# Two plain blocks for three at the start, spare matmuls between, and the last block stored by halves, in a recurrence followed by a two-layer feed-forward

## The chip, the cores and the metric

One core of a Trainium2 chip. The metric is the time of one execution on the device in microseconds (us), as the median of several. The kernel before takes 2353.7 us. The time of an execution is some 1.8 us longer than the span in its trace (2354.12 and 2352.3 for the profiled execution of the kernel before).

## The reference, cut to what matters

```python
# x, f_logit: (4, 6080, 256); lower_bound: (256,)
f = lower_bound + (1 - lower_bound) * sigmoid(f_logit)
for t in range(6080):
    h = f[:, t] * h + (1 - f[:, t]) * x[:, t];  y[:, t] = h
h = y.reshape(24320, 256) @ w_in       # (256, 2048)
out = (h - tanh(h)) @ w_out            # (2048, 256)
```

The weights come as 64-bit floats, which the kernel turns into float32 on the vector and scalar engines while it starts.

## The kernel before

The 24320 tokens are cut in blocks of 512 and one of 256. A block goes through the recurrence (two scans on the vector engine), the first product, an elementwise polynomial for h - tanh(h), and the second product. Most blocks do both products with seven instead of eight products of quarter matrices (sums of quarters before and after, on the vector engine). These need sums of the weights too, so the first blocks are "plain", with eight products, while the weights still come in.

```python
sizes = [TB, HB] + [TB] * (N // TB - 1)      # TB = 512, HB = 256
PLAIN, TURNED = 3, 2                          # blocks 0, 1, 2 are plain
```

An opening table gives the order of every step until the steady order begins; each word is an operation on one block or one piece of weights (W fetch, c.. conversion, tf/tx transposes of a block's inputs, sc scan, F first product, t q w a g the elementwise part, S second product, A and B sums of weights):

```python
before = """
    W.0 df.0 dx.0 ce.0 cr.0 cm.0 cx.0 W.1 cs.0 cb.0 tf.0 cw.0 df.1 W.2 tx.0 sg.0
    f1.0 cm.1 ce.1 f0.0 v0.0 cx.1 cr.1 dx.1 cb.1 v1.0 W.3 sc0.0 tf.1 sc1.0 sg.1
    ... (cut)
```

The end: after the last block's output is summed and transposed, four stores of 128 KB go out on the SyncE queue (pieces of 256 bytes). Then a flag is made that says whether any value was too large for the polynomial; every engine reads it and branches over a general program if it is zero:

```python
def give(j):
    nc.vector.transpose(out=osb..., in_=acc[j, "C"]...)
    for i in range(G):                        # G = 4
        nc.sync.dma_start(out=dst[i], in_=osb[i * H : (i + 1) * H, 0:n])
# ... after all blocks:
nc.vector.reduce_max(out=worst[:], in_=flags[:], axis=X)
nc.tensor.matmul(most[0:1, 0, 0:1], lhsT=worst[:], rhs=ones[:], ...)
nc.vector.tensor_copy(out=flag[:], in_=most[0:1, 0, 0:1])
# ... then
seen = nc.values_load(flag...)
with tc.If(seen != 0):
    general()
```

Of the kernel before, what the change touches and what calls it, by code (L numbers as in the profile page):

```python
# [31 lines left out]
def kernel(  # L32
# [41 lines left out]
    sizes = [TB, HB] + [TB] * (N // TB - 1)  # L74
    PLAIN, TURNED = 3, 2
# [170 lines left out]
    def fast(ctx):  # L246
# [253 lines left out]
        def give(j):  # L500
            n = sizes[j] // H
            osb = opool.tile([P, TB // H, H * KC], FP32, name="osb", tag="osb")
            nc.vector.transpose(
                out=osb[:, 0:n].rearrange("p j (a k) -> p j k a", k=KC),
                in_=acc[j, "C"][:, 0 : n * KC * H].rearrange(
                    "p (k j b) -> p j k b", k=KC, b=H
                ),
            )
            dst = out[starts[j] : starts[j] + sizes[j], :].rearrange(
                "(j b) (i c) -> i b j c", b=H, i=G  # L510
            )
            for i in range(G):
                nc.sync.dma_start(
                    out=dst[i],
                    in_=osb[i * H : (i + 1) * H, 0:n],
                )

# [65 lines left out]
        def load(j, s):  # L583

            nat = spot(j, ("fn", "xn")[s])
            (nc.sync, nc.scalar)[s].dma_start(
                out=nat[:, 0 : sizes[j] // P],
                in_=srcs[s][starts[j] : starts[j] + sizes[j], :].rearrange(
                    "(n p) d -> p n d", p=P
                ),  # L590
            )
            nats[j, s] = nat
# [17 lines left out]
        def squash_banks(j):  # L610
            u = midpool.tile([P, TB // H, KC, H], FP32, name="fT")[:, 0 : sizes[j] // H]
            for k in range(KC):
                nc.scalar.activation(
                    out=u[:, :, k, :], in_=nats[j, "banks", 0][k],
                    func=AF.Sigmoid, scale=-1.0,
                )
            chan[j, 0] = u
# [11 lines left out]

        def p_first(j, u, s):  # L630

            nb = sizes[j]
            if (j, u) not in plain:
                plain[j, u] = hpool.tile([P, 2, 2, TB], FP32, name="h", tag="h")
            banks = []
            for c in range(2):
                name = "AABD"[2 * s + c]
                if (j, u) == (1, 0):
                    name = "Q" + "abcd"[2 * s + c]
                pool = ps_a if name == "A" else ps_b  # L640
                bank = pool.tile([P, TB], FP32, name=name, tag=name)
                banks.append(bank[:, 0:nb])
                for k in range(KC):
                    nc.tensor.matmul(  # L644
                        bank[:, 0:nb],
                        lhsT=w_in[u][:, 2 * k + s, c * P : (c + 1) * P],
                        rhs=ys[j][:, k, 0:nb],
                        start=(k == 0),
                        stop=(k == KC - 1),
                    )  # L650
            plain[j, u, s] = dict(banks=banks)
# [9 lines left out]
        def p_square(j, u, s):  # L661
            t = p_temp(j, u, s, "t")
            for c in range(2):
                nc.scalar.activation(
                    out=t[:, c], in_=plain[j, u, s]["banks"][c], func=AF.Square
# [14 lines left out]
        def p_shrink(j, u, s):  # L680
            for c in range(2):
                nc.vector.tensor_tensor(  # L682
                    out=plain[j, u][:, s, c, 0 : sizes[j]],
                    in0=plain[j, u, s]["banks"][c], in1=p_temp(j, u, s, "q")[:, c],
                    op=ALU.mult,
# [10 lines left out]
        def p_second(j, u, s):  # L696

            ns = sizes[j] // P
            if u == s == 0:
                acc[j] = [  # L700
                    ps_b.tile([P, 2, D], FP32, name=f"Q{b}", tag=f"Q{b}")
                    for b in ("ab", "c", "ab")[j]
# [12 lines left out]
        def p_give(j):  # L715
# [19 lines left out]
            tx=lambda j: turn_by_matmul(j, 1) if j < TURNED else steps["tx"](j),  # L735
            sg=lambda j: squash_banks(j) if j < TURNED else steps["sg"](j),
# [15 lines left out]
        for name in ("ce", "cr", "cx", "cm", "cs", "cb", "cw"):  # L752
# [5 lines left out]
            W.0 df.0 dx.0 ce.0 cr.0 cm.0 cx.0 W.1 cs.0 cb.0 tf.0 cw.0 df.1 W.2 tx.0 sg.0  # L758
            f1.0 cm.1 ce.1 f0.0 v0.0 cx.1 cr.1 dx.1 cb.1 v1.0 W.3 sc0.0 tf.1 sc1.0 sg.1
            f0.1 cs.1 f1.1 F.0.0.0 tx.1 df.2 cw.1 cm.2 cr.2 v1.1 v0.1 sc1.1 t.0.0.0  # L760
            sc0.1 ce.2 F.1.0.0 q.0.0.0 cs.2 cx.2 F.0.0.1 a.0.0.0 dx.2 t.1.0.0 cb.2
            w.0.0.0 g.0.0.0 q.1.0.0 W.4 w.1.0.0 F.1.0.1 a.1.0.0 t.0.0.1 cw.2 w.0.0.1
            g.1.0.0 F.0.1.0 q.0.0.1 ce.3 cm.3 cx.3 a.0.0.1 t.1.0.1 cb.3 cr.3 g.0.0.1
            q.1.0.1 W.5 w.1.0.1 cs.3 t.0.1.0 F.0.1.1 a.1.0.1 q.0.1.0 cw.3 w.0.1.0
            g.1.0.1 cr.4 a.0.1.0 S.0.0.0 t.0.1.1 cm.4 g.0.1.0 q.0.1.1 w.0.1.1 cs.4
            F.1.1.0 a.0.1.1 S.0.0.1 t.1.1.0 ce.4 q.1.1.0 g.0.1.1 cx.4 a.1.1.0 w.1.1.0
            cb.4 F.1.1.1 g.1.1.0 W.6 cw.4 S.1.0.0 t.1.1.1 q.1.1.1 cm.5 cr.5 F.0.2.0
            a.1.1.1 ce.5 w.1.1.1 g.1.1.1 cx.5 cs.5 F.0.2.1 cb.5 t.0.2.0 tf.2 W.7 w.0.2.0
            cw.5 q.0.2.0 S.1.0.1 t.0.2.1 a.0.2.0 cr.6 ce.6 df.3 S.0.1.0 tx.2 w.0.2.1
            g.0.2.0 q.0.2.1 sg.2 a.0.2.1 S.0.1.1 cx.6 cm.6 f0.2 g.0.2.1 f1.2 dx.3 cs.6  # L770
            F.1.2.0 cb.6 F.1.2.1 t.1.2.0 cm.7 W.8 cw.6 q.1.2.0 w.1.2.0 S.1.1.0 a.1.2.0
            t.1.2.1 ce.7 cr.7 S.1.1.1 g.1.2.0 q.1.2.1 cs.7 w.1.2.1 F.0.3.0 a.1.2.1 cx.7
            v1.2 g.1.2.1 cm.8 cb.7 F.0.3.1 t.0.3.0 v0.2 q.0.3.0 cw.7 w.0.3.0 a.0.3.0
            S.1.2.0 t.0.3.1 sc1.2 cr.8 S.0.2.0 g.0.3.0 q.0.3.1 ce.8 w.0.3.1 a.0.3.1 cx.8
            S.1.2.1 sc0.2 g.0.3.1 F.1.3.0 cb.8 F.1.3.1 t.1.3.0 cs.8 q.1.3.0 w.1.3.0
            S.0.2.1 a.1.3.0 t.1.3.1 cw.8 w.1.3.1 A.0.1 q.1.3.1 a.1.3.1 S.0.3.0 g.1.3.0
            g.1.3.1 A.0.3 F.2.0.0 A.1.1 A.0.2 tx.3 F.2.0.1 t.2.0.0 tf.3 q.2.0.0 A.1.2
            w.2.0.0 a.2.0.0 S.1.3.0 t.2.0.1 A.0.0 sg.3 S.1.3.1 g.2.0.0 w.2.0.1 v0.3
            F.2.1.0 q.2.0.1 B.0.0 v1.3 f0.3 a.2.0.1 f1.3 o.1 sc1.3 S.0.3.1 t.2.1.0
            g.2.0.1 q.2.1.0 sc0.3 w.2.1.0 a.2.1.0 F.2.1.1 o.0 m13.3 g.2.1.0 m2.3 F.2.2.0  # L780
            A.1.0 t.2.1.1 B.0.1 q.2.1.1 m4.3 A.1.3 w.2.1.1 a.2.1.1 S.2.0.0 t.2.2.0
            g.2.1.1 q.2.2.0 w.2.2.0 a.2.2.0 F.2.2.1 g.2.2.0 S.2.0.1 B.0.2 t.2.2.1
            q.2.2.1 w.2.2.1 a.2.2.1 F.2.3.0 B.1.0 g.2.2.1 F.2.3.1 t.2.3.0 w.2.3.0
            q.2.3.0 B.0.3 t.2.3.1 a.2.3.0 q.2.3.1 g.2.3.0 w.2.3.1 a.2.3.1 g.2.3.1
        """
        left = {
            ("Qb", 1): ["S.2.1.0"],
            ("Qd", 1): ["S.2.1.1"],
            ("Qa", 2): ["S.2.2.0"],
            ("Qc", 1): ["S.2.2.1"],  # L790
            ("Qc", 2): ["S.2.3.0"],
            ("Qd", 2): ["S.2.3.1", "B.1.1", "B.1.2", "B.1.3"],
            ("Qb", 2): ["o.2"],
        }

        def open_by(words):
            for word in words:
                name, *at = word.split(".")
                opening[name](*[int(i) for i in at])

        with tc.manual_schedule():
            nc.vector.memset(zeros[:], 0.0)
            nc.vector.memset(ones[:], 1.0)
            nc.gpsimd.dma_start(
                out=lb[:], in_=lower_bound.rearrange("(p k) -> p k", k=KC)
            )
            make_identity(nc, ident[:])

            bank = ps_b.tile([P, 2, HB], FP32, name="B", tag="B")
            for _ in range(3):  # L810
                nc.tensor.matmul(
                    bank[:], lhsT=zeros[:, 0:P], rhs=zeros[:], start=True, stop=True,
                    skip_group_check=True,
                )
            nc.vector.tensor_scalar(
                out=om[:], in0=lb[:], scalar1=-1.0, scalar2=1.0,
                op0=ALU.mult, op1=ALU.add,
            )
            nc.vector.tensor_scalar_add(out=nom[:], in0=lb[:], scalar1=-1.0)
            open_by(before.split())  # L820
            fetch(PLAIN + 1)

# [6 lines left out]
            for cycle in range(PLAIN, NBLK + 3):  # L829
                for name, u, at in turns:  # L830
                    j = cycle + at
                    if j == PLAIN - 1:
                        open_by(left.get((name, u), ()))
                    if not PLAIN <= j < NBLK:
                        continue
                    if u is None:
                        if (j, name) == (PLAIN, "m4"):
                            continue
                        steps[name](j)
                        if name == "tx" and j + 1 < NBLK and j > PLAIN:  # L840
# [3 lines left out]
            nc.vector.reduce_max(out=worst[:], in_=flags[:], axis=mybir.AxisListType.X)  # L844
            most = ps_b.tile([P, 2, HB], FP32, name="most", tag="D")
            nc.tensor.matmul(
                most[0:1, 0, 0:1], lhsT=worst[:], rhs=ones[:], start=True, stop=True
            )
# [130 lines left out]
```

## Time and profile before

| | kernel before |
|---|---|
| time, median of three | 2353.72 us |
| span in the trace | 2352.3 us |
| first useful product on TensorE | 14.44 us |
| last product ends | 2342.4 us |
| from there to the end ("the tail") | 9.98 us (9.9 in the prediction) |

TensorE is busy 99% of the span. A table like this is read from the two ends: in the middle TensorE never waits, so its time there is fixed by the number of products, and what can be won is a block's products, the opening, and the tail. The lines are shown and read in the prediction.

### The profile page before, as it was taken

To read this page: it belongs to the slowest core of one execution; us is meant where nothing else is said; L and a number is where in the kernel's file an instruction comes from. 1 tells how busy PE (TensorE), PEld (TensorE's weight loads), DVE (VectorE), ACT (ScalarE), POOL (GpSimd) and SP (SyncE) were. 2 spreads that over 40 slices of the span, in tenths; PEclk is the share of its full clock that TensorE was granted. 3 is DMA by queue.
4 is the path that set the end of the run, shared out by engine and by line. 5 is a ranking of instruction groups with operands and counts; after the bars stand their busy time and mean duration, and the time that the engine had idled before them with its cause. 6 is when DMAs were issued, how large, how long until landed. Compare 5 with 4: busy or idle time off the path is not lost.

```text
span 2352.3 us, 28494 instructions
## 1 busy us (share of the span) xinstructions
PE 2329.0 (99%) x10626; PEld 2019.8 (86%) x10626; DVE 2105.5 (90%) x2437; ACT 1794.1 (76%) x2681; POOL 1.4 (0%) x7
## 2 busy tenths in 40 slices
PE   8999999999999999999999999999999999999998
PEld 5768888888888888888888888888888888888887
DVE  8939998999899998999999998999989998999987
ACT  7648777777877777777777777777787777777775
POOL 0000000000000000000000000000000000000000
PEclk9999999999999999999999999999999999999999
DMA  5221111111211112111211112111111112111101
GB/s 171 50 35 28 27 39 34 37 27 28 46 33 31 27 32 41 36 28 27 44 29 37 27 27 46 36 28 28 36 37 36 28 28 45 30 34 28 27 10 29
DMA packets 296803, 85.04 MB, mean 36 GB/s; under 512 B 289744, under 2 KB 292560, under 8 KB 296656
## 3 DMA queue, kind: packets, MB, share of 16 engines
q1 hardware_dynamic: 295824, 82.35, 16.8%
q8 instruction: 85, 1.39, 0.2%
q10 hardware_dynamic: 800, 0.79, 0.1%
q14 instruction: 62, 0.51, 0.1%
q0 software_dynamic: 32, 0.00, 0.0%
HBM read 58.20 MB, written 24.90 MB: 35 GB/s over the span
## 4 chain that ended last, share of the span: by engine, by line
PE 98%; DVE 1%; DMA 0%; ACT 0%; issue 0%; DVEq 0%; POOLq 0%
PE A L383 26%; PE D L383 13%; PE Qd L466 13%; PE Qa L466 13%; PE Qb L466 13%; PE B L383 7%; PE Qc L466 7%; PE A L644 1%; PE Qa L706 1%; PE Qb L706 1%; PE B L644 1%; PE Qc L706 1%; PE D L644 1%; DVE q L676 0%; DMA lb<-in_lower_bound_dram 0%; DVE h L682 0%
## 5 line engine op out<-in xcount | busy, mean ns | idle before, releaser
L383 PE MATMUL A<-T,w_in 128*128 128x256 f32 x2160 | 547.0, 379 | 0.0
L383 PEld LDWEIGHTS A<-T,w_in 128*128 128x128 f32 x2160 | 410.3, 190 | 56.1 <-ACT B L395 0.3
L427 DVE TENSOR_TENSOR h<-h,q 128x1024 f32<-128x1024 f32 x360 | 428.1, 1221 | 3.1
L421 DVE SCALAR_TENSOR_TENSOR q<-q,t 128x1024 f32<-128x1024 f32 x360 | 430.5, 1217 | 0.0
L414 ACT ACTIVATE q<-t 128x1024 f32<-128x1024 f32 x360 | 374.4, 1053 | 44.3 <-DVE h L427 41.5
L411 ACT ACTIVATE t<-h 128x1024 f32<-128x1024 f32 x360 | 380.2, 1056 | 5.3 <-DVE h L398 2.6
L432 ACT ACTIVATE junk<-t 128x1024 bf16<-128x1024 f32 x360 | 379.7, 1055 | 1.5
L446 DVE TENSOR_TENSOR Tg<-h 128x1024 f32<-128x1024 f32 x360 | 340.7, 946 | 6.4
L466 PE MATMUL Qb<-h,w_out 128*128 128x256 f32 x1440 | 340.2, 379 | 0.0
L466 PEld LDWEIGHTS Qb<-h,w_out 128*128 128x128 f32 x1440 | 273.6, 190 | 37.2
L395 ACT COPY h<-B 128x512 f32<-128x512 f32 x180 | 104.8, 582 | 149.7 <-PE B L383 92.8
L466 PE MATMUL Qd<-Tg,w_out 128*128 128x256 f32 x720 | 214.1, 379 | 0.0
L466 PE MATMUL Qa<-Tg,w_out 128*128 128x256 f32 x720 | 214.1, 379 | 0.0
L466 PE MATMUL Qd<-h,w_out 128*128 128x256 f32 x720 | 214.1, 379 | 0.0
L466 PE MATMUL Qa<-h,w_out 128*128 128x256 f32 x720 | 214.1, 379 | 0.0
L398 DVE TENSOR_TENSOR h<-D,r 128x512 f32<-128x512 f32 x180 | 124.2, 690 | 100.4 <-PE D L383 99.4
L395 ACT COPY h<-A 128x512 f32<-128x512 f32 x180 | 104.9, 583 | 133.5 <-PE A L383 122.4
L398 DVE TENSOR_TENSOR h<-A,r 128x512 f32<-128x512 f32 x180 | 123.6, 687 | 82.1 <-PE A L383 50.8
L383 PE MATMUL A<-y,w_in 128*128 128x256 f32 x720 | 185.7, 380 | 0.0
L383 PE MATMUL D<-T,w_in 128*128 128x256 f32 x720 | 185.7, 380 | 0.0
L395 ACT COPY r<-A 128x512 f32<-128x512 f32 x180 | 104.9, 583 | 105.1 <-PE A L383 105.1
L383 PE MATMUL B<-y,w_in 128*128 128x256 f32 x720 | 184.8, 379 | 0.0
(114 smaller groups left out, 3173.7 us busy)
## 6 DMA issues: line engine op xcount, KB each, us to landing
fn<-in_f_logit_dram SPq DMA_DIRECT2D x184, 128.0 KB, 3.2
xn<-in_x_dram SPq DMA_DIRECT2D x184, 128.0 KB, 3.3
out_dram<-osb SPq DMA_DIRECT2D x180, 128.0 KB, 2.8
raw<-in_moe_w_in_dram SPq DMA_DIRECT2D x8, 512.0 KB, 5.2
raw<-in_moe_w_out_dram SPq DMA_DIRECT2D x8, 512.0 KB, 5.0
out_dram<-osb SPq DMA_DIRECT2D x2, 512.0 KB, 3.4
xn<-in_x_dram ACTq DMA_DIRECT2D x1, 512.0 KB, 4.0
fn<-in_f_logit_dram SPq DMA_DIRECT2D x1, 512.0 KB, 6.2
```

What stands on the lines that cost most here:

```text
L383: nc.tensor.matmul(ps[:, c], lhsT=w_in[u][:, slot, c * P : (c + 1) * P], rhs=mixes[j][right], start=start and c == 0, stop=True, skip_grou ...
L395: nc.scalar.copy(out=dst, in_=piece(n, bank))
L398: nc.vector.tensor_tensor(out=piece(n, "h")[:, q], in0=piece(n, bank), in1=piece(n, r), op=ALU.add)
L411: nc.scalar.activation(out=half(n, i, "t"), in_=half(n, i), func=AF.Square)
L414: nc.scalar.activation(out=half(n, i, "q"), in_=half(n, i, "t"), func=AF.Square, scale=RA, bias=RB,)
L421: nc.vector.scalar_tensor_tensor(out=q, in0=q, scalar=RC, in1=t, op0=ALU.add, op1=ALU.mult)
L427: nc.vector.tensor_tensor(out=h, in0=h, in1=q, op=ALU.mult)
L432: nc.scalar.activation(out=junk[:, :, :, 0 : st[n]["hb"]], in_=t, func=AF.Relu, bias=-TINY, accum_out=flags[:, 2 * n + i : 2 * n + i + 1],)
L446: nc.vector.tensor_tensor(out=o, in0=a, in1=b, op=ALU.subtract)
L466: nc.tensor.matmul(acc[j, part][:, r, 0 : st[n]["hb"]], lhsT=w_out[u][:, slot, c * P : (c + 1) * P], rhs=piece(n, right)[:, q, c], start=( ...
L644: nc.tensor.matmul(bank[:, 0:nb], lhsT=w_in[u][:, 2 * k + s, c * P : (c + 1) * P], rhs=ys[j][:, k, 0:nb], start=(k == 0), stop=(k == KC - 1),)
L706: nc.tensor.matmul(acc[j][i // 2][:, i % 2].rearrange("p (k m) -> p k m", k=2), lhsT=plain[j, u][:, s, c, i * P : (i + 1) * P], rhs=w_out[ ...
```

## The change

Its intent: one plain block fewer, so that one more block has seven products for eight; a smaller first block, so that TensorE starts earlier; the next block already interleaved with the last plain work; spare matmuls of zeros so that TensorE's clock stays up; and a shorter end. Beside this, the first inputs are all loaded by SyncE's queue, the lower bound by ScalarE's, and the sigmoid table is loaded at the start. The core of the diff (the new table of about 330 words, bank names and helpers are cut):

```diff
-    sizes = [TB, HB] + [TB] * (N // TB - 1)
-    PLAIN, TURNED = 3, 2
+    sizes = [HB] + [TB] * (N // TB)
+    PLAIN, TURNED = 2, 2
...
+        def end(j):
+            for half, slot, r in ((0, 2, 1), (1, 1, 0)):
+                nc.vector.tensor_tensor(
+                    out=C[:, slot], in0=acc[j, 3][:, r, 0:hb], in1=C[:, slot], op=ALU.add)
+                turn_out(j, (slot,))
+                send(j, half)                 # four stores of 64 KB, SyncE queue
...
+            K1.7 W.0 df.0 ce.0 cr.0 dx.0 cm.0 tf.0 cx.0 W.1 cs.0 tx.0 sg0.0 cb.0 K1.4
+            sg1.0 df.1 v0.0 f0.0 cw.0 f1.0 v1.0 dx.1 ce.1 tf.1 sc1.0 cx.1 sc0.0 W.2 cr.1
+            cm.1 tx.1 sg1.1 cb.1 sg0.1 cs.1 F.0.0.0 f0.1 v1.1 f1.1 dx.2 v0.1 K1.4 cw.1
+            t.0.0.0 sc0.1 q.0.0.0 F.0.0.1 w.0.0.0 W.3 sc1.1 cr.2 K1.2 a.0.0.0 t.0.0.1
+            F.1.0.0 ...
...
+        def keep_busy(n):                     # the word K1.n
+            for _ in range(n):
+                nc.tensor.matmul(busy[:], lhsT=zeros (bf16), rhs=zeros (bf16, 512 wide), ...)
...
-            nc.gpsimd.dma_start(out=lb[:], ...)
+            nc.scalar.dma_start(out=lb[:], ...)
...
+                        if (name, j) == ("o1", NBLK - 1):
+                            tc.mark_branch_hint_location("general", "LikelyTaken")
+                            nc.vector.reduce_max(out=worst[:], in_=flags[:], ...)
+                        if j == NBLK - 1 and name in ("o4", "otr"):
+                            if name == "o4":
+                                sum_up()      # flag: matmul and ScalarE copy, now early
+                                end(j)
+                            continue
...
+                        if (name, j) == ("o3", NBLK - 1):
+                            turn_out(j, (0, 3))
-    with tc.If(seen != 0):
+    with tc.If(seen != 0, label="general"):
```

## The prediction

> **What bounds the kernel now.** I read the page first, then the chain of waits in order of time, then the opening, the change of method and the end instruction by instruction.
>
> ```profile
> PE 2329.0 (99%) x10626; PEld 2019.8 (86%) x10626; DVE 2105.5 (90%) x2437; ACT 1794.1 (76%) x2681; POOL 1.4 (0%) x7
> ```
>
> TensorE is busy 99% of a span of 2352.3 us, so the steady part has nothing to win except matmuls that go away. The vector engine at 90% is the next bound, close behind. The chain of waits gives the period of a block of 512 tokens by seven products:
>
> ```profile
> 258.28 1.73 PE A L383 x8
> ...
> 354.97 1.73 PE A L383 x8
> ```
>
> These are two equal places two blocks apart: 96.69 us, 48.35 us for a block. It agrees with the counts: 224 matmul records a block, about 0.216 us apart. The reader is to see that every microsecond that is not 48.35 times a number of blocks lies at the two ends. The waits of TensorE in the first 200 us, and the busy times of the engines in four stretches (columns: stretch, its length, then PE, PEld, DVE, ACT and POOL busy with counts, clock, DMA share, GB/s):
>
> ```profile
> PE B L825 <- DVE h L682: 4.0, 1, 4.0
> PE A L644 <- DVE y L227: 3.8, 1, 3.8
> PE Qa L644 <- DVE y L227: 2.4, 1, 2.4
> ```
>
> ```profile
> 14.44:37.85 23.41, 19.95 (x52) 10.17 (x53) 20.36 (x30) 18.23 (x31) 0.00 (x0) 0.93 0.65 141
> 37.85:137.90 100.05, 100.05 (x369) 69.73 (x367) 86.30 (x136) 66.60 (x113) 0.00 (x0) 1.00 0.28 62
> 137.90:147.90 10.00, 6.03 (x14) 4.14 (x14) 6.75 (x8) 3.74 (x6) 0.00 (x0) 0.66 0.38 65
> 147.90:193.00 45.10, 45.10 (x210) 39.45 (x209) 20.54 (x25) 25.42 (x42) 0.00 (x0) 1.00 0.11 21
> ```
>
> All those waits are for the vector engine. It is the limit from 14.44 to 37.85 us and again at the change of method near 140 us; between and after, TensorE never waits, and from 147.9 to 193 us the vector engine stands idle more than half the time. The opening and the change of method, from the timeline:
>
> ```profile
> 6.35 0.17 DVE L815 TENSOR_SCALAR om<-lb 128x2 f32<-128x2 f32 x1 [4.93 <-DMA lb<-in_lower_bound_dram]
> ...
> 7.60 1.28 ACT L613 ACT_TABLE_LOAD   x1
> ...
> 14.44 5.40 PE L644 MATMUL A<-y,w_in 128*128 128x512 f32 x8 [3.83 <-DVE y L227]
> ...
> 141.89 2.08 PE L825 MATMUL B<-zeros 128*128 128x512 f32 x2 [3.97 <-DVE h L682]
> ...
> 143.76 1.91 PE L383 MATMUL A<-y,w_in 128*128 128x256 f32 x4
> ```
>
> The first useful product starts at 14.44 us. The last plain product of the opening table begins at 136.04 us and lasts 1.88; the bank B is cleared only at 141.89, and the first of the seven products runs at 143.76 at half clock. The end, from the chain:
>
> ```profile
> 2340.64 1.74 PE Qd L466 x8
> 2342.38 0.02 issue
> 2342.40 0.70 DVE C L498
> 2343.10 0.02 issue
> 2343.13 1.25 DVE osb L503
> ...
> 2345.18 0.15 DVE flag L849
> ```
>
> TensorE ends at 2342.4; 9.9 us remain. Of these 2.0 are the sum and the transposition, 0.8 the flag, and some 7 the last four stores and the branch over the general program.
>
> **What the Trainium skill says.** "TensorE: Matmul & The Clock Gate", Part 1, "What's actually happening": after an idle window of about 3.4 us the array runs at half clock until it has been busy for about as long. The trace agrees: after the two waits of 3.8 and 4.0 us the granted clock falls (0.93 and 0.66 in the rows above), and eight 512-wide records take 5.40 us where the chain later shows 3.43. "ScalarE: Activation LUTs", "What ACT_TABLE_LOAD costs", gives 1283 ns for the load itself; the trace has 1.28 us, twice, the second just before the first sigmoid. "DMA: Bandwidth & Descriptors", "SWDGE vs HWDGE vs iDMA", calls transfers from the scalar engine faster to set up than those from GpSimd; the trace has only the GpSimd one for the lower bound, 5.1 us from issue to landing. "Runtime: NRT & Kernel Launch", "Instruction fetch mechanics": a taken branch to a page that is not loaded waits for its fetch by DMA; in the last 6.8 us nine instruction packets move, which agrees.
>
> **The change part by part.**
>
> *A block turned from plain to seven products.* Plain block of 512: per quarter of the weights the first layer is 16 records of 512 columns (3.43 for eight in the chain, so 6.87) and the second 32 of 256 (6.9); four quarters are 55.1 us. Seven products: 48.35. The new kernel has 46 such blocks for 45, one plain 512 for two, and the 256 (27.6) in both. TensorE gains 6.75 us.
>
> *What TensorE's end consists of, before.* 45 x 48.35 = 2175.8, plain work 55.1 x 2 + 27.6 = 137.8, together 2313.6. The remainder to 2342.4 is 28.8: start 14.44; waits 2.45 and 1.0; two pairs of transposes between products 0.6; 6.0 from the end of the plain products (137.75) to the first of the seven; half clock 1.7 (14.77 to 18.2, half of it lost) and 2.1 (143.76 to 147.9). Sum 28.3, so the books close.
>
> *Start.* 256 tokens first: the two scans cost about 0.65 each for 1.15, the factors v 0.4 for 0.65. The vector engine's work ahead of the first product falls from 7.9 to 6.4 us by my sum of durations. The lower bound comes through the scalar engine's queue and its two small results are made there, so the vector engine need not wait until 6.35; fewer bytes (1.0 MB for 1.5) are asked for ahead of the first weights; the sigmoid table is loaded in the idle start, which takes 1.28 us off the scalar engine's way. From about 5.3 us: 5.8 of vector work less memsets gives 10.4 if nothing stalls, 11.4 if the first weights still land at 6.1. I take 10.8: 3.6 gained.
>
> *Opening from there.* I summed the durations of each word of the new table: between the first product and the first of the seven products the vector engine has 68.2 us of work, TensorE 72.7 with its spare matmuls. Up to the first second-layer product it is 19.4 against 18.4. The same sum for the kernel before gives 20.4 vector us where the window shows 20.36, so the sums hold; there that stretch took 23.4, the vector engine busy 87%. At the same share the new stretch takes 22.3, so about 4 us of wait or spare, and I add 1 for half clock that the spare matmuls (zeros, bfloat16, 0.22 us each, 11 early and 6 later) don't prevent: 5.
>
> *Change of method.* In the new table the second layer of the plain block still runs among the first products of the block after, and the clear of B comes while others wait; 0.9 for the clear and 2 for waits, where before it was 6.0 + 2.1. New remainder: 10.8 + 5 + 2.9 = 18.7. TensorE's end: 46 x 48.35 + 55.1 + 27.6 + 18.7 = 2325.5, 16.9 earlier.
>
> *End.* The last block's sums r=1 and r=0 are made, turned and stored apart, two of the four transpositions done before. First store possible 0.8 us after the last product for 2.0. But eight issues of some 0.4 to 0.5 us stand for four on one queue, and the same count of small packets moves, so not all of the 1.2 arrives. The flag is made while the sums wait, so its load and the branch no longer come last, hinted or not. I take 8.2 for 9.9: 1.7 gained.
>
> Sum: 6.75 (the block) + 3.6 (start) + 6.5 (opening and change of method: 14.4 before, 7.9 after) + 1.7 (end) = 18.6. Span 2352.3 - 18.6 = 2333.7; the time stood 1.4 us above the span, so 2335 us.
>
> **The rivals.** First: the vector engine becomes the bound. The plain block that goes had 18.6 us of vector work (eight times 1.13 + 1.2) beside its recurrence for 55.1 of TensorE; a block by seven products has about 44 for 48.35 (915 us busy in 1000 of the steady part), and all the conversion of the weights and their sums stay. From the first product to the end of the new table I count 110.3 vector us for 115.9 TensorE us. The slack that the old kernel had from 147.9 to 193 us is gone. For it: the rows at 14.44 and 137.9. Against it: 5.6 us are still free in the table, and steady blocks give back 4 us each. If it idles 10% of the opening, TensorE waits 6 to 10 us more: 2341 to 2345. Second: the order in the new table is so good that the waits vanish and the spare matmuls keep the clock full: 4 to 6 us less, 2329 to 2331. Third: the last stores are bound by their packets and by the issuing queue, and the halves bring nothing: 1.7 us more, 2337. Fourth: the spare matmuls sit before useful ones and delay them; 17 by 0.22 are 3.7 us at most at full clock, of which I have most counted in the 5.
>
> **Range and chances.** Mostly the vector engine in the opening decides: minus 6 to plus 7 around 2335, 2329 to 2342. For 2% the time would have to fall by 47 us; all that is not useful work in the old kernel is 28.8 + 9.9 us, and with the 6.75 the whole is 45.5. So faster by over 2%: 0.01; within 2%: 0.985; slower: 0.005.
>
> **What would show it.** The first first-layer product near 10.8 us; no granted clock under 0.9 near 140 us; waits of TensorE in the first 150 us of about 5 to 7 us in all; the period of 48.35 us unchanged; TensorE's end near 2325.5 and about 8 us behind it. Wrong, if the period changes, if waits for the vector engine in the first 150 us exceed 12 us, or if the last 8 us are still 10.

## The result, and the profile after

The changed kernel takes 2335.9 us (median of 4 runs, 2334.3 to 2336.5), the kernel before in the same rounds 2353.65. The ratio is 0.992, 95% interval 0.9903 to 0.9937, which is within 2%, as forecast. A ratio here is the mean time of one kernel's runs over that of the other's of the same rounds, so not quite the ratio of the medians. The prediction was 2335. But two of its terms were wrong, in opposite directions, as the trace shows: TensorE ends at 2321.5 us where 2325.5 was predicted, and the tail is 13.2 us where 8.2 was.

The first line of the page after:

```profile
PE 2318.4 (99%) x10669; PEld 2024.6 (87%) x10669; DVE 2121.2 (91%) x2450; ACT 1800.4 (77%) x2685; POOL 0.7 (0%) x6
```

The waits of TensorE in the first 200 us after, all of them; the second is for the memset at the very start:

```profile
PE Qa L623 <- DMA fn<-in_f_logit_dram: 1.5, 1, 1.5
PE B L849 <- DVE ones L875: 1.5, 1, 1.5
```

Before, the same view had three waits of 2.4 to 4 us and one of 1.0 us for the vector engine. After, there is none for it but that memset. The busy times of the engines in stretches of the new opening (stretch, length, then PE, PEld, DVE, ACT and POOL, clock, DMA share, GB/s):

```profile
12.43:30.93 18.50, 18.50 (x64) 11.23 (x63) 18.23 (x25) 16.27 (x28) 0.00 (x0) 1.00 0.82 185
30.93:90.00 59.07, 59.07 (x234) 44.11 (x233) 56.44 (x81) 41.95 (x67) 0.00 (x0) 1.00 0.30 88
90.00:100.00 10.00, 10.00 (x48) 8.81 (x47) 7.67 (x17) 6.18 (x11) 0.00 (x0) 1.00 0.01 2
100.00:145.00 45.00, 45.00 (x210) 39.44 (x209) 43.48 (x60) 38.25 (x61) 0.00 (x0) 1.00 0.32 65
```

From the first product (12.43) to the first second-layer product (30.93) the vector engine is busy 18.23 of 18.50 us, 99%. In the old opening the same stretch was busy to 87%. Up to the scans of the second block the vector engine sets the pace, as the first rival feared, but it hardly idles, and TensorE, filled up with spare matmuls, shows no wait.

The timeline of the new opening, cut to the lines that matter:

```profile
5.28 0.43 DVE L134 TENSOR_SCALAR e<-raw 128x512 int32<-128x512 int32 x1 [3.88 <-DMA raw<-in_moe_w_in_dram]
...
12.43 1.89 PE L678 MATMUL A<-y,w_in 128*128 128x256 f32 x8
...
14.62 2.45 DVE L227 TENSOR_TENSOR_SCAN y<-f,y,v 128x512 f32<-128x512 f32 x2
...
17.18 1.88 PE L678 MATMUL Qa<-y,w_in 128*128 128x512 f32 x4
...
84.36 1.02 PE L859 MATMUL B<-zeros 128*128 128x512 f32 x2
85.22 1.03 PE L383 MATMUL A<-y,w_in 128*128 128x256 f32 x4
```

The scans of the second block end at 17.07 us (14.62 + 2.45), and its first product starts at 17.18. The change of method at 84 us, which cost 6 us of waiting and 2 of slow clock before, costs only the 0.86 us of the clear. The period of a block is the same as before, 48.34 us, between equal places in the chain of waits:

```profile
285.78 1.73 PE A L383 x8
...
334.12 1.73 PE A L383 x8
```

The end, from the timeline: the vector engine's last work, then the row of SyncE's queue, the eight last stores put together.

```profile
2320.89 0.77 DVE L512 STREAM_TRANSPOSE osb<-C 128x256 f32<-128x256 f32 x2
...
2321.58 0.39 DVE L535 TENSOR_TENSOR C<-Qd,C 128x256 f32<-128x256 f32 x1
...
2322.80 0.45 DVE L512 STREAM_TRANSPOSE osb<-C 128x256 f32<-128x256 f32 x1
```

```profile
2322.48 7.24 SPq L521 DMA_DIRECT2D out_dram<-osb  x8
```

Before, the four stores were issued in 2.17 us, also from the timeline:

```profile
2344.40 2.17 SPq L513 DMA_DIRECT2D out_dram<-osb  x4
```

The halves do go out earlier after TensorE's end: the first at 1.0 us for 2.0. But eight issues take 7.24 us, so the last one is out at 8.2 us after TensorE's end; before it was out at 4.2. After its last issue SyncE still loads the flag, branches and runs a row of closing waits. From the end of that issue to the end of the program are 5.0 us here, 5.8 before, and 5.0 to 6.6 in all fourteen traces. In the changed kernel the last store has landed at 9.6 us, while SyncE is back from its branch at 11.3. So the tail follows SyncE's last issue. One by one, as the trace has them (start after TensorE's last product, length):

```
 before  +2.04 0.32   +2.68 0.32   +3.05 0.51   +3.61 0.60
 after   +0.97 0.32   +1.33 0.44   +1.83 2.20   +4.07 0.45
         +4.62 0.41   +5.07 0.46   +5.58 2.14   +7.76 0.45
 16 KB instruction packets on queue 8:
 before  +5.62 for 1.35            +9.18 for 0.96
 after   +1.96 for 1.64            +5.79 for 1.53
```

Six issues take 0.32 to 0.46 us, two take 2.2. Both slow ones lie over a large instruction fetch. The DMA view (queue, packets, MB, share of the engines' time) shows the same: first the 2.3 us of the first slow issue in the new kernel, then the 2.4 us of the four issues in the kernel before, which have no packet of queue 8:

```profile
q1 hardware_dynamic: 525, 0.13, 25.2%
q8 instruction: 1, 0.02, 4.5%
q14 instruction: 2, 0.02, 3.3%
```

```profile
q1 hardware_dynamic: 880, 0.22, 41.2%
q14 instruction: 1, 0.01, 0.8%
```

Whose fetches are they? The 16 KB packets of queue 8 come every 27.6 us (median) in the steady part, and TensorE issues 448 recorded instructions in 48.35 us, so 256 in 27.6: that would be 64 bytes for each. At the end, the first of the two large packets starts 1.0 to 2.0 us after TensorE's branch in all fourteen traces, wherever that branch is. So I take them for TensorE's, which is an inference. That an issue is held where it meets such a packet also shows away from the end. In the steady part of the changed kernel's trace SyncE issues 500 transfers. The 28 during which a packet of queue 8 moves take 0.72 us on average and up to 1.64; the other 472 take 0.47, and none over 0.86 (counted in the packed trace). In the new kernel the flag is made before the last sums, so TensorE branches at 0.93 us after its last product (before: 3.74) and its two fetches fall among the stores.

### The profile page after: what moved, and what is told of

It is laid out like the page before. It is cut to its first block, busy times and chain, and to the rows that moved or that the text cites. A ratio compares the mean times of both kernels' runs of the same rounds, so it can differ in the third digit from the quotient of the medians.

```text
span 2334.7 us, 28635 instructions
## 1 busy us (share of the span) xinstructions
PE 2318.4 (99%) x10669; PEld 2024.6 (87%) x10669; DVE 2121.2 (91%) x2450; ACT 1800.4 (77%) x2685; POOL 0.7 (0%) x6
## 4 chain that ended last, share of the span: by engine, by line
PE 99%; DMA 0%; SPq 0%; DVE 0%; issue 0%; DVEq 0%
PE A L383 27%; PE Qa L466 14%; PE Qb L466 14%; PE D L383 14%; PE Qd L466 14%; PE Qc L466 7%; PE B L383 7%; PE Qc L745 1%; PE Qa L745 1%; PE Qb L745 1%; PE A L678 1%; PE D L678 0%; PE Qd L678 0%; DMA xn<-in_x_dram 0%; PE B L678 0%; PE Qc L678 0%
## 5 line engine op out<-in xcount | busy, mean ns | idle before, releaser
L383 PE MATMUL A<-T,w_in 128*128 128x256 f32 x2208 | 558.8, 379 | 0.0
L383 PEld LDWEIGHTS A<-T,w_in 128*128 128x128 f32 x2208 | 419.5, 190 | 57.0
L427 DVE TENSOR_TENSOR h<-h,q 128x1024 f32<-128x1024 f32 x368 | 437.3, 1219 | 3.1
L421 DVE SCALAR_TENSOR_TENSOR q<-q,t 128x1024 f32<-128x1024 f32 x368 | 439.8, 1215 | 0.0
L414 ACT ACTIVATE q<-t 128x1024 f32<-128x1024 f32 x368 | 382.9, 1053 | 46.3 <-DVE h L427 43.4
L411 ACT ACTIVATE t<-h 128x1024 f32<-128x1024 f32 x368 | 388.6, 1056 | 3.1 <-DVE h L398 0.3
L432 ACT ACTIVATE junk<-t 128x1024 bf16<-128x1024 f32 x368 | 388.2, 1055 | 1.5
L446 DVE TENSOR_TENSOR Tg<-h 128x1024 f32<-128x1024 f32 x368 | 347.8, 945 | 6.3
L466 PE MATMUL Qb<-h,w_out 128*128 128x256 f32 x1472 | 347.7, 379 | 0.0
L383 PE MATMUL D<-y,w_in 128*128 128x256 f32 x736 | 188.9, 379 | 0.0
```

The costliest lines, as they stand in the source:

```text
L383: nc.tensor.matmul(ps[:, c], lhsT=w_in[u][:, slot, c * P : (c + 1) * P], rhs=mixes[j][right], start=start and c == 0, stop=True, skip_grou ...
L411: nc.scalar.activation(out=half(n, i, "t"), in_=half(n, i), func=AF.Square)
L414: nc.scalar.activation(out=half(n, i, "q"), in_=half(n, i, "t"), func=AF.Square, scale=RA, bias=RB,)
L421: nc.vector.scalar_tensor_tensor(out=q, in0=q, scalar=RC, in1=t, op0=ALU.add, op1=ALU.mult)
L427: nc.vector.tensor_tensor(out=h, in0=h, in1=q, op=ALU.mult)
L432: nc.scalar.activation(out=junk[:, :, :, 0 : st[n]["hb"]], in_=t, func=AF.Relu, bias=-TINY, accum_out=flags[:, 2 * n + i : 2 * n + i + 1],)
```

## The experiments

All outputs are right. Each kernel had five timed runs; the kernel before, in the same rounds, had medians from 2353.78 to 2354.02. Runs 1 to 4, 5 to 8 and 9 to 12 shared one chip each, three chips in all. "TensorE's end" and "tail" are of each one's profiled execution.

| run | time, median | range | TensorE's end | tail |
|---|---|---|---|---|
| changed, first trace | 2335.9 | 2334.3-2336.5 | 2321.5 | 13.2 |
| new opening, old end | 2334.23 | 2333.6-2335.3 | 2323.6 | 9.8 |
| whole store, early flag | 2335.01 | 2333.63-2336.01 | 2323.7 | 10.5 |
| halves, late flag, no hint | 2335.75 | 2335.52-2336.7 | 2322.5 | 11.3 |
| no hint | 2338.29 | 2336.62-2338.4 | 2323.7 | 12.7 |
| halves on two queues | 2334.18 | 2333.92-2335.13 | 2322.1 | 11.1 |
| no spare matmuls | 2336.97 | 2336.02-2337.66 | 2323.1 | 12.1 |
| product ahead of transposes | 2339.1 | 2337.92-2340.15 | 2325.3 | 13.1 |
| old opening, new end | 2357.15 | 2355.58-2359.8 | 2341.9 | 13.4 |
| changed, again | 2336.43 | 2335.71-2338.65 | 2324.0 | 12.8 |
| two queues, flag after sums | 2333.08 | 2333.03-2334.57 | 2323.6 | 9.1 |
| the same, no spare | 2334.04 | 2333.46-2334.28 | 2322.9 | 9.4 |
| the same, whole store | 2333.41 | 2333.0-2334.86 | 2323.1 | 9.5 |

The five times of one kernel spread by 0.8 to 4.2 us (those of the control by 2.9), so two medians about 1 us apart are not told apart here.

My theory for the end: the early flag brings the branch's fetches into the stores. Rivals: eight issues are too many in any case; the hint makes the fetches. For the opening: the vector engine's chain to the second block's scans decides, against the moment of the first product.

**1. New opening, old end.**

```diff
-  early reduce_max, hint, sum_up(), end(j), turn_out(j, (0, 3))
+  one sum, one transposition, four stores; then reduce_max, matmul, copy as before
```

> The new opening with the old end: one sum, one transposition, four stores, flag last, no hint. The changed kernel's trace has TensorE ending at 2321.5 us and 13.2 us after it, where the kernel before had 9.9. Theory A (the new end costs what the opening won too much): TensorE ends at 2321.5 again, 9.9 us behind it, span near 2331.4, time near 2332.6, 3.3 below the changed kernel. Rival (the longer tail only moved there because the opening shifted the stores against the instruction fetches): the tail stays at 12 to 13 us and the time near 2336.

The tail is 9.8 us and the four issues take 2.18 us (SyncE's row of the timeline, below): theory A. The time is 1.6 us above the number expected, because TensorE ended at 2323.6, not 2321.5; that is the subject of the control below.

```profile
2325.66 2.18 SPq L521 DMA_DIRECT2D out_dram<-osb  x4
```

**2. Whole store, early flag and hint kept.**

```diff
-                                end(j)
-                            turn_out(j, (0, 3))
+  (the ordinary o4 and give, four stores of 128 KB)
```

> The changed kernel with the early flag and the hint, but one sum, one transposition and four stores of 128 KB. Theory A1 (an issue on the SyncE queue stalls some 1.7 us when it meets one of the two large instruction fetches of TensorE's branch): one of four issues is stalled, issues end about 5.7 us after TensorE, tail 10.5 to 11.5, time about 2333.5 to 2334. Rival A2 (only the number of issues counts, each has its chance of a slow one): no stall, tail 9 to 9.5, time near 2332.

Tail 10.5. The four issues take 3.29 us; two are slow (1.30 and 1.04 us) and each lies over or beside a packet of queue 8 (at 1.98 for 1.27, and 5.80 for 1.09 us after TensorE's end; the slow issues began at 2.40 and 4.28 us). The second slow one ends at 5.3, ahead of the second of these packets; a packet of 8 KB on queue 14 lies over it (at 4.31 for 0.48), but whether that one holds it I did not test. The tail fits theory A1.

**3. Halves, late flag.**

```diff
-  reduce_max at o1 and sum_up() ahead of end(j)
+  reduce_max and sum_up() after the last transposition
-  the hint and the label of the branch
```

> The changed kernel with the halves, but the flag made after the last transposition, so that TensorE's branch comes about 1.5 us later. Theory A1 (collision of issues with the fetches): the eight issues run at 0.45 us each and end about 4.6 us after TensorE, the tail is 9.5 to 10.5, time about 2332.5 to 2333.5. Rival A2 (eight issues are too many whatever else happens): two issues stall again or the tail stays at 12.5 us and more, time 2335 to 2337.

Tail 11.3: between the two numbers. Seven of the eight issues take 0.32 to 0.47 us, and only the last, at 4.37 us, takes 1.65; the fetch starts at 4.44. So the same eight issues run without the two stalls when the fetch is later, which speaks against A2, and one stalls again where it still meets it. (The hint went out too; run 4 shows that it doesn't make the stalls.) The time alone (2335.75) would not have shown it: the range overlaps that of the changed kernel. The eight together, from SyncE's row of the timeline, take 5.05 us for 7.24:

```profile
2323.42 5.05 SPq L521 DMA_DIRECT2D out_dram<-osb  x8
```

**4. No hint.**

```diff
-                            tc.mark_branch_hint_location("general", "LikelyTaken")
-    with tc.If(seen != 0, label="general"):
+    with tc.If(seen != 0):
```

> The changed kernel without the branch hint. If the hint does nothing here: time and tail as in the changed kernel, within 0.5 us, TensorE's branch about as long. If it shortens the branch (the trace has 4.13 us for TensorE's branch against 4.70 before): the branch takes 4.7 us again; the tail changes by 0.6 us at most, as SyncE ends last. If the hint itself makes the fetches that stall the issues: the tail falls to about 10 us and the time to about 2333.

The two slow issues are there without the hint (1.76 and 2.07 us, over the fetches at 1.96 and 5.31), so the hint doesn't make them. From TensorE's branch to its next instruction are 3.71 us without and 4.18 with; for SyncE 2.47 and 2.48. In these two traces the hint shortens no branch that matters. Yet the timed median is the highest of its batch, 1.9 us over that of the changed kernel in the later batch, on another chip; the ranges overlap, and the ratios to the kernel before (0.9929 and 0.9925) are not told apart. What the hint is worth stays open.

**5. Halves on two queues.**

```diff
+            queue = nc.scalar if half == 1 else nc.sync
-                nc.sync.dma_start(
+                queue.dma_start(
```

> The changed kernel with the last half's four stores issued by ScalarE's queue, the first half's by SyncE's. Theory A1 (issues one behind the other on one queue, with stalls): at most one stall on each queue, SyncE's issues end near 4.5 us after TensorE, tail 9.5 to 10.5, time about 2332.5 to 2333.5. Rival (the transfers themselves, 2048 packets of 256 bytes, set the end): tail stays at 12.5 us and more.

Tail 11.1, a miss upward: both queues met the first fetch. The third issue of SyncE takes 2.07 us and the second of ScalarE 1.68. So a stall isn't of one queue: an issue of either engine can be held while the fetch runs.

**6. No spare matmuls.**

```diff
-            K1.7 W.0 ...  cb.0 K1.4 ... v0.1 K1.4 cw.1 ... cr.2 K1.2 a.0.0.0
+            W.0 ...  cb.0 ... v0.1 cw.1 ... cr.2 a.0.0.0
```

> The changed kernel without the 17 spare matmuls of the opening. Theory B (they only fill waits and keep the clock full): without them TensorE runs part of the first 25 us at half clock, and its first products of 256 and 512 columns take up to twice as long; time 1 to 3.5 us longer. Rival (the vector engine sets the pace until the scans of the second block at 17 us, so a slow clock is hidden): no change within 0.5 us; or they delay useful products: up to 1.6 us shorter.

1.1 us above the changed kernel's 2335.9, inside theory B's range, at its lower edge. TensorE's end is 1.6 us later than in the first trace, but earlier than in most other traces with spare matmuls. Its first 16 records take 4.75 us, so the clock was low, and the second block's product began at 18.67 us. Read this together with the control.

**7. First product ahead of the second block's transposes.**

```diff
-            cm.1 tx.1 sg1.1 cb.1 sg0.1 cs.1 F.0.0.0 f0.1
+            cm.1 F.0.0.0 tx.1 sg1.1 cb.1 sg0.1 cs.1 f0.1
```

> The changed kernel with the first eight product records (256 tokens) ahead of the transposes of the second block's x on TensorE, so that the first product starts at about 11.2 us for 12.43. If the moment of the first product is what the opening costs (as the prediction's sum has it): TensorE ends up to 1.2 us earlier. Theory C (the vector engine's chain to the second block's scans sets the opening, and the first product is only a filler): no gain, and a loss of up to 1.5 us, as those transposes and with them the factors and scans come 1 to 1.7 us later.

The slowest of the new openings: 2339.1 us. The timeline (TensorE and the scan):

```profile
12.09 3.49 PE L678 MATMUL A<-y,w_in 128*128 128x256 f32 x8
15.42 0.63 PE L623 MATMUL Qc<-ident,xn 128*128 128x128 f32 x4
...
18.56 2.45 DVE L227 TENSOR_TENSOR_SCAN y<-f,y,v 128x512 f32<-128x512 f32 x2
...
20.96 1.88 PE L678 MATMUL Qa<-y,w_in 128*128 128x512 f32 x4
```

The first product starts at 12.09 us, and the scan of the second block moves from 14.62 to 18.56. Part of this is the clock, which was halved in this trace from 11.90 to 15.32 (the product takes 3.49 us for 1.89). Beside run 1, whose clock was low at the same time, the first product is 1.7 us earlier (13.78 there), the scan 2.5 later (16.02) and TensorE's end 1.7 later (2323.6). Theory C.

**8. Old opening, new end.**

```diff
-  give() as it was; flag after all blocks
+  turn_out, send, end(j), sum_up(), the hint: all in the kernel before
```

> The old opening (1280 plain tokens) with the new end. Theory A: the end costs 3.3 us more than the old one wherever it stands: TensorE ends at 2342.4, tail about 13.2, span about 2355.6, time about 2357. Rival (the fetches fall differently here, as their place depends on the count of TensorE's instructions): tail near 10 us, time near 2353.7 or below.

2357.15 us against 2353.93: by the medians the new end by itself costs 3.2 us, though the ratio, 1.0012 with an interval of 0.9998 to 1.0026, doesn't quite exclude no change. The trace is clearer: TensorE ends at 2341.9 for 2342.4, and the tail is 13.4 for 10.0; two issues take 2.21 and 1.77 us. Theory A.

**9. The changed kernel again, as a control.**

> The changed kernel itself once more, beside the next three on the same chip. Expected 2335 to 2337 us. Where its trace shows the clock dropping to half near 12 us, as four of the experiments' traces did, TensorE ends near 2323.8 us; where it doesn't, near 2321.8. The tail is 13 us either way.

2336.43 us, tail 12.8. In this trace the clock does drop, and TensorE ends at 2324.0. The busy times and clock of the same stretch in this trace, and in the first trace:

```profile
12.50:16.00 3.50, 3.50 (x14) 3.03 (x14) 1.85 (x3) 1.97 (x4) 0.00 (x0) 0.51 1.27 232
```

```profile
12.50:16.00 3.50, 3.50 (x18) 2.72 (x18) 3.30 (x5) 2.92 (x5) 0.00 (x0) 1.00 1.31 212
```

It is the same program. Where the clock is halved, TensorE delivers the second block's transposes late, and the vector engine, which waits for them, is busy 1.85 of 3.5 us for 3.30. The second block's inputs also land later here (its first transposes start at 10.76 for 9.94), so the 2.5 us between the two ends are not the clock's alone. The same program keeps its clock in one execution and loses it in another. Where a trace has several steps of the clock in its opening, they lie 3.41 us or a multiple of it apart. In the new opening with spare matmuls, TensorE was busy 27 to 53% of the 3.41 us before each of the seven falls, and 59% or more of every such stretch of the first 20 us after which the full clock stayed (counted in the packed traces on the grid of each one's own steps). So it matters how that grid falls on TensorE's waits for the inputs.

What holds is this: from the first product of the second block to TensorE's end are 2304.3 us in all ten traces of the new opening with spare matmuls, within 0.1, among them the first trace (17.18 to 2321.5), run 7 (20.96 to 2325.3) and this one (19.63 to 2324.0); without them they are 2304.4 and 2304.8. In that stretch TensorE does not wait at all. What varies in the opening is the time until the second block's first product, which waits for its scans and for the records ahead of it on TensorE.

**10. Halves on two queues, flag copied after the last transposition.**

```diff
+            queue = nc.scalar if half == 1 else nc.sync
...
-                                sum_up()            # with the ScalarE copy
-                                end(j)
+                                most = sum_up()     # without it
+                                end(j)
+                                nc.vector.tensor_copy(out=flag[:], in_=most[0:1, 0, 0:1])
```

> The changed kernel with the halves on two queues (SyncE, ScalarE) and the flag copied by the vector engine after its last transposition, so that TensorE's branch begins about 2.5 us after its last product and its first large fetch at about 3.5, when all eight stores are issued (the last at about 3.6). If the collision is the whole matter: no issue over 0.8 us, tail 8.2 to 9, 4 to 5 us less than the changed kernel, time 2331 to 2332.5. If the small packets or the waits at the end set it: tail 10 us or more.

No issue takes over 0.48 us, as the trace has them. The timeline, SyncE's four and ScalarE's four:

```profile
2324.62 3.13 SPq L522 DMA_DIRECT2D out_dram<-osb  x4
```

```profile
2325.41 1.97 ACTq L522 DMA_DIRECT2D out_dram<-osb  x4
```

The last is out 4.1 us after TensorE's end, where it was 8.2. The first fetch, at 3.59, meets only the last issue of each queue, when most of their work is done, and slows neither (0.48 and 0.32 us). The tail is 9.1 us, 0.1 more than I expected at most, and the time 2333.08 us, 0.6 over the range I gave (its trace has the low clock and TensorE's end at 2323.6). The later flag alone (run 3) had a tail of 11.3, the two queues alone (run 5) 11.1. The time is 3.3 us under that of the changed kernel on the same chip, with ranges that don't overlap, and the lowest median of all runs: ratio to the kernel before 0.9912, interval 0.9899 to 0.9926.

**11. The same without spare matmuls.**

> The run before with the spare matmuls taken out. Without them the clock came up at 16.6 us in one trace and TensorE ended at 2323.3, against 2321.8 to 2323.9 with them[...]. If that is all: 0 to 1.5 us slower than the run before, not 3.

(The times that this expectation quotes from traces stand 0.25 us later than the document's, as do the prediction's 14.77 and 18.2 us for the clock: another origin.)

2334.04 for 2333.08, the means 2333.9 and 2333.55; the ranges overlap. The 17 spare matmuls are worth at most about 1 us. With them the second block's product began between 17.18 us (clock never dropped) and 19.63 (dropped), without them at 18.67 and 18.08: they win in some executions and lose in others. In the control that product began 3.6 us after the start of the scans (16.07 to 19.63), without spare matmuls 2.3 and 2.0 us after: at a low clock, as I read it, the useful records and the spare ones together last longer than the scans.

**12. The same with a whole store, two of the four on each queue.**

> The run with two queues, but one sum, one transposition and four stores of 128 KB, two on each queue. If halving is worth anything by itself once no issue is stalled: 0.5 to 1.2 us slower than with halves, as the first store goes out 1.1 us later. If not: the same within 0.4 us.

2333.41 for 2333.08, the means 2333.75 and 2333.55: the same within 0.4 us. Once nothing is stalled, halving the last store has no gain that these runs can show, though it goes out 1.1 us earlier (tail 9.5 for 9.1 in the traces). SyncE's last issue ends 1.2 us earlier with the whole store (2.9 for 4.1), but its load of the flag and its branch take 1.5 us longer in that trace (4.7 for 3.2).

## Why the prediction was right, and where only in sum

The time was met by luck: two terms were wrong by 4 and 5 us and cancelled. Of the signs that the prediction named, the period and the clock near 140 us came true. The first product, the waits and TensorE's end did not. One of its signs of being wrong came: the last stretch is not 8 us, nor still 10, but 13.2.

**The block turned to seven products: right.** The period is unchanged (48.34 us), the count of blocks is 46, and the 2304.3 us close: 46 x 48.345 is 2223.9, the plain block of 512 is 55.1, the rest of the one of 256 is 27.6 less the two products ahead of it (3.4), and the clear 0.9, together 2304.1.

**The start: wrong by 1.6 us, and not the term to look at.** The first weights' conversion starts at 5.28 us as estimated and the first scans end at 10.77, but the first product waits on TensorE behind the second block's transposes until 12.43. Run 7 shows that to take it earlier makes the kernel slower. The sum itself doesn't close either: 5.3 and 5.8 are 11.1, not 10.4. The lower bound, by ScalarE's queue, landed 1.8 us after its issue, for 5.1. The prediction counted the opening from the first product; it is the second block's scans that count.

**Waits in the opening: the term that was mis-sized, 5 and 2 us for none.** The step was "At the same share the new stretch takes 22.3, so about 4 us of wait or spare". The share of 87% was carried over from the old order, which was bound by other waits. In the new order the stretch took 18.5 us at 99%, with 18.2 us of vector work where 19.4 were counted. The 2 us of waits at the change of method are absent too. Instead of 18.7 us beside useful work, the first trace has 14.9: 12.43 of start, 1.3 of spare matmuls (from their start to the next useful one), 0.9 of clear, and some 0.3 that I can't assign. A loss by half clock was allowed for with 1 us; it is absent in the first trace and part of 2.5 us in the control.

**The end: wrong in sign, 13.2 us for 8.2.** The step that failed is "The flag is made while the sums wait, so its load and the branch no longer come last". On TensorE they come earlier, but among the stores, and there the fetches of the branch hold two of the eight issues for some 1.7 us each beyond their 0.45. The last store is out at 8.2 us after TensorE's end where my estimate gives 4.4 (0.8 and eight times 0.45), which is 3.8 of the 5.0 us of error. The rest is that on SyncE they still come last: its load of the flag, branch and closing waits follow its last issue and take 5.0 us. So even without a stall 8.2 was out of reach: 4.4 and 5.0 are 9.4, and run 10 has 9.1. Runs 8, 1 and 10 show it from three sides: the new end put on the old opening has a tail of 13.4, the old end on the new opening has a tail of 9.8, and with the issues out of the fetches' way 9.1.

So the predicted gain of 18.6 us of span was 6.75 + 3.6 + 6.5 + 1.7, and the measured 17.6 is 20.9 to TensorE's end less 3.2 in the tail (rounded). The 1.4 us from span to time, taken from a median and a span of different executions, are 1.8. The time hit the forecast because an opening 4 us better met a tail 5 us worse. Of the rivals, the second (no waits, full clock) is right for the opening of the first trace: TensorE ends 4.0 us earlier than forecast, of the 4 to 6 it gave. The third (halves bring nothing) came true, and worse; the issuing queue is the cause, as it said, but by held issues, and no run shows the count of packets to matter. The fourth (spare matmuls delay useful ones) fits executions with a low clock, which runs 6 and 11 do not settle.

## What to carry to other kernels

When two terms of a forecast meet in one number, check each at its own place in the trace: here at TensorE's last product. In an opening, find the step after which the bound engine never waits again, and count until there; the first product may be only a filler. And work that is moved earlier "off the path" can collide with what it now lies beside: a branch's instruction fetches held the last stores.

## What the Trainium skill lacked or had wrong

- "Runtime: NRT & Kernel Launch", "Instruction fetch mechanics", says of crossing a block of instructions that its cost is mostly hidden, and of a taken branch that it stalls on the fetch. No page has a figure for a branch that must fetch, or says that a fetch holds up others. Here a taken branch takes 2.5 to 4.8 us to the next instruction of an engine that has to fetch, and DMA issues of SyncE and of ScalarE that meet a 16 KB fetch take 1.6 to 2.2 us for 0.32 to 0.5 us (runs 3, 5 and 8, and the changed kernel; 0.8 to 1.3 in the control and run 2, and some that met one in runs 2, 5 and 10 were not slowed).
- "TensorE: Matmul & The Clock Gate", "What's actually happening", ties the half clock to an idle window of about 3.4 us, though it also says that the clock follows how busy the engine has been. Here the clock fell at 11.1 to 12.5 us in the control and in six experiments (runs 1, 2, 4, 7, 10 and 12), though TensorE had transposes and spare matmuls in the 7 us before, with no wait over 2.6 us; in three of the traces with the same spare matmuls (the first, runs 3 and 5) it didn't fall. By what share of busy time it stays up, no page says; here 27 to 53% lost it and 59% kept it.
- No page has a figure for what a branch hint is worth; run 4 doesn't settle it.
